# A new order for gates, key flips and route: one route tile with one key flip, gate copies later

## The chip, the cores and the metric

The kernel runs on one core of one Trainium2 chip. The metric is the device time of one execution in microseconds (us); lower is better. Engines are named as in the profile: PE is TensorE (PEld its weight loads), DVE is VectorE, ACT is ScalarE, POOL is GpSimd, SP is SyncE, which here only issues transfers.

## The reference

Eight batches of packed attention feed a mixture of experts with one expert per token, all in float32:

```
s  = scale * p @ k.T;  a = softmax(s);   p_packed = a @ v      # 32 packed queries per head
s2 = scale * q @ p_packed.T;  out = softmax(s2) @ p_packed      # 8 x 8 heads x 576 x 64
x  = out as rows (4608 x 512)
xn = x / (|x| + 1e-6);  en = emb / (|emb| + 1e-6)
logits = xn @ en.T / tau;  expert = argmax(logits);  gate = softmax(logits)[expert]
out[rows of e] = gate * (relu(x @ w1[e]) @ w2[e])               # 512 -> 1024 -> 512
```

## The kernel before

Each batch (576 tokens) has two parts. The attention part, `att_main(b)`, ends with the second softmax (`att2`), whose result is `AT`, the attention weights, transposed, as a high and a low half (`high`, `low`). The expert part, `ffn(b)`, guesses one expert for the whole batch, multiplies with its weights, and leaves tokens of other experts to a second pass at the end (none is taken in these inputs).

**Two programs woven by hand.** `ffn` is a generator that stops after every few matmuls, 56 stops for a usual batch: n = 0 to 15 are the hidden layer (`hidden`), n = 16 to 39 the transposed output rows of the last 320 tokens (line 943, four blocks `mt`), n = 40 to 55 the output tiles of the first 256 tokens (line 961, two tiles `c` of eight steps `f`). At each stop the loop at the end of the function takes one step of the next batch's attention (`step_att`), and from n = 28 (`GATE`) one step of this batch's gates (`gates_main`). For the first batch, which has 61 stops, an order written by hand, `PLAN`, says for each stop which steps to take: "a" is the second batch's attention, "k" one of its query flips, "g" gates, "r" the first batch's route, "w" and "W" the split of a weight tile on POOL or DVE, "q" and "s" steps of the first batch. The stop only sets where an instruction stands in its own engine's queue. Each engine then runs its queue in order, at its own pace.

**The steps around the change.** In the usual batch, attention's 32nd step is `turn(1)` on DVE; step 34 issues `low(1)`; steps 36 to 40 are the keys of the batch after next: `packers` and four `flip`s on DVE (three transposes each, lines 288 to 290); steps 41 to 45 are `route`. `route` has five tiles of tokens. Each takes a PSUM buffer `pt` of a pool of two, has six matmuls on PE (line 682), a small reduction on DVE (line 691) and a sum of squares on ACT (line 698), which frees the buffer. The reduction and the sum of one tile are issued one step after its matmuls.

`gates` makes the gate of each token of the batch: an inverse square root by small operations, mostly on POOL, then reciprocal and exponential on DVE and ACT (lines 744 to 755), then 16 small copies on ACT that spread the gates of the last 320 tokens (`spread_tail`, line 770). `store_tail` multiplies the transposed output by these (line 1269) and issues its output transfers; `turn_tail` (line 1260) brings each of the four `mt` blocks from PSUM on DVE.

The last attention (eighth batch) has no keys behind it, so its route comes five steps sooner. In the second batch (`early`) route starts one step after `turn(1)`, and its tiles alternate with the flips.

Of the kernel before, what the change touches and what calls it, by code (L numbers as in the profile page):

```python
# [23 lines left out]
def kernel(  # L24
# [12 lines left out]
    nc = tc.nc  # L37
# [3 lines left out]
    NG = H // HB  # L41
# [180 lines left out]
    def alternate(a, b):  # L222

        while a or b:
            for g in (a, b):
                if g:
                    try:
                        yield next(g)
                    except StopIteration:
                        a, b = (None, b) if g is a else (a, None)  # L230

    def idle(n):
        for _ in range(n):
            yield
# [190 lines left out]
    def rows_split(x, g):  # L425
        split([x.ppx[:, m, g, : HB * D] for m in range(2)], x.pp4[g].rearrange("p h d -> p (h d)"))
# [133 lines left out]
    def att2(x, after=None, first=False, early=False):  # L560

        def eng(name, hf):
            i = ("S0", "S1", "N0", "N1", "L0", "L1").index(name + str(hf))
            return nc.gpsimd if first and ENG[i] == "p" else nc.vector

        AT = sb.tile([P, 2, NG, S], F32R, name="AT", tag="AT")
        x.AT = AT
        NB = HS // 32
        both = slice(0, NG)
        sts, mxs, sums = [], [], []  # L570
        ats = x.ats = []

        def rows_of(t, gs):
            return t[:, gs].rearrange("p g (a j) -> p g a j", j=32)

        def spread(t, gs):
            n = gs.stop - gs.start
            return t[:, gs].unsqueeze(3).broadcast_to([P, n, NB, 32])

        def unpack(hf, gs=both):  # L580
            if gs.start == 0:
                sts.append(sb.tile([P, NG, HS], F32, name="st", tag="st", bufs=2))
            for g in range(gs.start, gs.stop):
                nc.vector.transpose(sts[hf][:, g], x.s2[hf][g])  # L584

        def biggest(hf, gs=both):
            if gs.start == 0:
                mxs.append(sm.tile([P, NG, NB], F32, name="mx2", tag="mx2", bufs=1))
            nc.vector.tensor_reduce(  # L589
                mxs[hf][:, gs], rows_of(sts[hf], gs), axis=AX.X, op=ALU.max  # L590
            )

        def shift(hf, gs=both):
            t = rows_of(sts[hf], gs)
            eng("S", hf).tensor_tensor(out=t, in0=t, in1=spread(mxs[hf], gs), op=ALU.subtract)  # L595

        def expo(hf, gs=both):
            nc.scalar.activation(sts[hf][:, gs], sts[hf][:, gs], AF.Exp, scale=SCALE)  # L598

        def total(hf, gs=both):  # L600
            if gs.start == 0:
                sums.append(sm.tile([P, NG, NB], F32, name="s2", tag="s2", bufs=1))
            t = sums[hf][:, gs]
            nc.vector.tensor_reduce(t, rows_of(sts[hf], gs), axis=AX.X, op=ALU.add)  # L604
            nc.vector.tensor_scalar(out=t, in0=t, scalar1=1e-9, scalar2=None, op0=ALU.add)
            nc.vector.reciprocal(t, t)

        def norm(hf, gs=both):
            t = rows_of(sts[hf], gs)
            eng("N", hf).tensor_tensor(out=t, in0=t, in1=spread(sums[hf], gs), op=ALU.mult)  # L610

        def turn(hf, gs=both):
            if gs.start == 0:
                if first and hf:
                    at = sb.tile([P, NG, HS], F32, name="at1", tag="ot", bufs=1)
                else:
                    at = sb.tile([P, NG, HS], F32, name="at", tag="at")
                ats.append(at)
            nc.vector.transpose(  # L619
                ats[hf][:, gs].rearrange("p g s -> p (g s)"),  # L620
                sts[hf][:, gs].rearrange("p g s -> p (g s)"),
            )

        def high(hf, gs=both):
            nc.scalar.copy(AT[:, 0, :, hf * HS : (hf + 1) * HS], ats[hf])  # L625

        def low(hf, gs=both):
            cs = slice(hf * HS, (hf + 1) * HS)
            eng("L", hf).tensor_tensor(
                out=AT[:, 1, :, cs], in0=ats[hf], in1=AT[:, 0, :, cs].bitcast(F32),  # L630
                op=ALU.subtract,
            )

        def softmax():
            order = (
                (unpack, 0), (biggest, 0), (shift, 0), (unpack, 1), (biggest, 1), (total, 0),
                (shift, 1), (norm, 0), (turn, 0), (total, 1), (low, 0), (norm, 1), (turn, 1),
            )
            if first:
                names = dict(  # L640
                    U=unpack, B=biggest, S=shift, X=expo, T=total, N=norm, R=turn, H=high, L=low
                )
                groups = {"": both, "a": slice(0, 1), "b": slice(1, 2)}
                order = [(names[t[0]], int(t[1]), groups[t[2:]]) for t in ORDS.split()]
            for step, hf, *gs in order:
                step(hf, *gs)
                if step is shift and not first:
                    expo(hf)
                if step is turn and not first:
                    high(hf)  # L650
                yield
            if first:
                return
            if early:

                steps = route(x)
                yield next(steps)
                low(1)
                yield
                yield from alternate(steps, after)  # L660
                return
            yield
            low(1)
            yield from idle(2)
            if after:
                yield from after

        yield from softmax()


# [61 lines left out]
        x.cnt = cnt  # L732


    def gates(x, eng=nc.vector):
        lg, ss = x.lg, x.ss
        y = sm.tile([P, NC5], F32, name="gy", tag="gy", bufs=1)
        for n, _ in enumerate(rsqrt(ss, y, "g", eng)):
            if n % 3 == 2:
                yield  # L740
        eng.tensor_tensor(out=y, in0=y, in1=ss, op=ALU.mult)
        eng.tensor_scalar(out=y, in0=y, scalar1=1e-6, scalar2=None, op0=ALU.add)
        yield
        nc.vector.reciprocal(y, y)
        nc.vector.tensor_tensor(
            out=lg, in0=lg, in1=y.unsqueeze(2).broadcast_to([P, NC5, E]), op=ALU.mult
        )

        nc.scalar.activation(lg, lg, AF.Exp)
        yield  # L750
        gate = sm.tile([P, NC5], F32, name="gate", tag="gate")
        nc.vector.tensor_reduce(gate.unsqueeze(2), lg, axis=AX.X, op=ALU.add)
        nc.vector.tensor_scalar(out=gate, in0=gate, scalar1=1e-9, scalar2=None, op0=ALU.add)
        yield
        nc.vector.reciprocal(gate, gate)  # L755

        x.gate = gate
        x.gt = sm.tile([P, NBT], F32, name="gt", tag="gt", bufs=1)
        yield
        for n, _ in enumerate(spread_tail(x.gt.unsqueeze(2), gate.unsqueeze(2), nc.scalar.copy)):  # L760
            if n % 4 == 3:
                yield
# [91 lines left out]
    def ffn(x, store, late=False, after=None, end=False):  # L854
# [99 lines left out]
        for c in range(NCT):  # L954

            w = 256 if end and c == NCT - 1 else 512
            for at in range(0, 512, w):
                pf = ps.tile([P, 512], F32, name="pf", tag="pf")
                for f in range(NF):
# [8 lines left out]
                    yield  # L968
                    if f == 0 and turning:
                        turn_tail(*turning.pop())  # L970
                    if f > 1:
                        next(tail, None)
                    if f == STF and last:
                        store(*last.pop(0))
# [50 lines left out]
    def att_main(b):  # L1025
        x = bat[b]
# [28 lines left out]
            load_w2(x, x.e, nc.gpsimd)  # L1055
        yield from second
        x.soft = True
        if b > 1:
            yield from route(x)
        if b == B - 1:  # L1060
            yield from idle(2)
            counts(x)
# [1 line left out]
    def begin():  # L1064
# [3 lines left out]
        x = bat[0]  # L1068
# [147 lines left out]
        yield  # L1216
        for g in range(NG):
            rows_split(x, g)
            yield
        x.begun = True  # L1220

    def keys_main(b):
        if b < B:
# [2 lines left out]

    def gates_main(b):
        x = bat[b]
        yield from gates(x, nc.gpsimd)
        hit = sm.tile([1, E], F32, name="hit", tag="hit")  # L1230
        nc.vector.tensor_tensor(out=hit, in0=x.cnt, in1=x.sel, op=ALU.mult)
        nc.vector.tensor_reduce(rest_f[:, b : b + 1], hit, axis=AX.X, op=ALU.add)

    def store_main(b):
# [60 lines left out]

    PLAN = (
        "qssq", "sssssssss", "sss", "ss", "ss", "ssG", "", "sG", "ssa", "ssa",
# [5 lines left out]
    )  # L1303
    DBL = 8
    LAG = 2

# [5 lines left out]
    with tc.manual_schedule():  # L1312
# [41 lines left out]
        for b in range(B):  # L1354
            after = bat[b + 1] if b + 1 < B else None
# [24 lines left out]
    with tc.If(n_rest > 0):  # L1380
        with tc.For_i(0, B, 1) as b:
            nb = nc.values_load(rest_i[0:1, ds(b, 1)], min_val=0, max_val=S)
            with tc.If(nb > 0):
                x = Batch()
# [97 lines left out]
```

## Time and profile before

| | |
|---|---|
| median of 3 runs | 490.4 us (488.78 to 492.2) |
| the profiled execution's own time | 490.11 us |
| its span, first to last instruction | 488.4 us |
| mean granted TensorE clock | 0.946 of full |
| PE, DVE, ACT, POOL busy | 90%, 62%, 45%, 36% |

The span and the trace are of the profiled execution; 1.7 us of its time lie outside the span. The trace's times are from the span's start. PEclk is the share of TensorE's full clock that was granted; it has two levels here, 1.0 (2.4 GHz) and 0.5 (1.2 GHz).

### The profile page before, as it was taken

How to read it: one execution, taken by the hardware profiler on the slowest of the kernel's cores; microseconds unless marked ns; L12 is line 12 of the kernel's file. 1: busy time of each engine (PE TensorE's matmuls, PEld its weight loads, DVE VectorE, ACT ScalarE, POOL GpSimd, SP SyncE). 2: the span in 40 equal slices, each digit the busy share in tenths (PEclk: the TensorE clock that was granted, in tenths of full speed). 3: DMA queues.
4: the chain of work that ended last, by engine and by line, in shares of the span. 5: the costliest groups of instructions: out<-in, count | busy, mean ns of one | idle time of the engine just before them, and what ended most of it. 6: DMA issues, size and time to landing. Idle time of an engine off the chain costs nothing.

```text
span 488.4 us, 10755 instructions
## 1 busy us (share of the span) xinstructions
PE 439.7 (90%) x3890; PEld 375.9 (77%) x3891; DVE 300.9 (62%) x874; ACT 219.2 (45%) x580; POOL 177.9 (36%) x303
## 2 busy tenths in 40 slices
PE   8799888999869996999959999599987999699994
PEld 5547778699857995788947989469976799679993
DVE  5487777477753887357963677547874488345330
ACT  2467425562246623474244721556234662437230
POOL 2456370343504353153512617044440535317200
PEclk9999997999979999899979999799997999799997
DMA  7999897758872588636973489725888203521022
GB/s 216 291 295 256 228 274 246 171 129 242 335 197 70 140 261 307 147 93 179 319 255 79 129 225 349 202 49 137 246 315 196 74 21 141 206 54 44 1 53 51
DMA packets 48860, 88.23 MB, mean 181 GB/s; under 512 B 11992, under 2 KB 30488, under 8 KB 48800
## 3 DMA queue, kind: packets, MB, share of 16 engines
q1 hardware_dynamic: 40512, 57.96, 44.8%
q0 software_dynamic: 8000, 29.43, 16.9%
q8 instruction: 32, 0.52, 0.5%
q14 instruction: 28, 0.23, 0.2%
q10 hardware_dynamic: 288, 0.08, 0.1%
HBM read 78.00 MB, written 9.44 MB: 179 GB/s over the span
## 4 chain that ended last, share of the span: by engine, by line
PE 59%; DVE 19%; DMA 8%; POOL 6%; issue 4%; ACT 1%; SPq 1%; DVEq 0%; ACTq 0%; POOLq 0%
PE pf L915 18%; PE pf L961 17%; PE pt L682 6%; PE pf L943 6%; DMA nat<-in_q 4%; DMA nat<-in_v 3%; PE pt L263 3%; PE pt L833 3%; POOL rq_t L106 2%; PE pt L388 2%; DVE st L584 2%; POOL rq_t L115 2%; DVE mx L589 2%; DVE s L604 2%; DVE st L595 2%
## 5 line engine op out<-in xcount | busy, mean ns | idle before, releaser
L809 POOL TENSOR_TENSOR w2s<-w2r,w2s 128x512 fp32r<-128x512 f32 x61 | 78.4, 1291 | 166.9 <-ACT w2s L808 86.0
L943 PE MATMUL pf<-hT,w2s 128*128 128x320 f32 x768 | 122.3, 315 | 0.0
L943 PEld LDWEIGHTS pf<-hT,w2s 128*128 128x128 f32 x768 | 115.4, 191 | 3.6 <-issue 3.3
L915 PE MATMUL pf<-AT,G 128*128 128x288 f32 x720 | 103.7, 298 | 0.1
L961 PE MATMUL pf<-w2s,hT 128*128 128x512 f32 (+1 forms) x408 | 101.1, 394 | 0.0
L915 PEld LDWEIGHTS pf<-AT,G 128*128 128x128 f32 x720 | 97.3, 188 | 4.7 <-issue 2.8
L961 PEld LDWEIGHTS pf<-w2s,hT 128*128 128x128 f32 x408 | 73.7, 196 | 18.4 <-issue 5.9
L682 PE MATMUL pt<-ppx,AT 128*128 128x264 f32 (+1 forms) x240 | 45.6, 336 | 33.6 <-ACT at L698 31.0
L918 DVE SCALAR_TENSOR_TENSOR hT<-pf,hT 128x288 fp32r<-128x288 f32 x128 | 56.4, 446 | 25.0 <-ACT hT L917 23.8
L682 PEld LDWEIGHTS pt<-ppx,AT 128*128 128x128 f32 (+1 forms) x240 | 41.5, 225 | 39.4 <-ACT at L698 33.4
L917 ACT ACTIVATE hT<-pf 128x288 fp32r<-128x288 f32 x128 | 51.4, 414 | 39.9 <-PE pf L915 38.4
L808 ACT CAST w2s<-w2r 128x512 fp32r<-128x512 f32 x64 | 39.1, 625 | 17.1 <-issue 15.2
L698 ACT ACTIVATE at<-pt 128x512 f32<-128x512 f32 (+1 forms) x40 | 23.9, 597 | 38.2 <-DVE lg L691 38.0
L847 DVE TENSOR_TENSOR G<-pt,G 128x512 fp32r<-128x512 f32 x28 | 19.4, 692 | 32.0 <-ACT G L846 32.0
L598 ACT ACTIVATE st<-st 128x576 f32<-128x576 f32 (+1 forms) x17 | 11.2, 660 | 51.5 <-DVE st L595 28.1
L770 ACT COPY gt<-gate 32x2 f32<-32x2 f32 (+1 forms) x128 | 24.6, 192 | 9.7 <-DVE gate L755 8.2
L691 DVE TENSOR_REDUCE lg<-pt 128x8 f32<-128x16 f32 (+1 forms) x40 | 5.8, 158 | 33.2 <-PE pt L682 33.2
L278 POOL TENSOR_TENSOR ppx<-pp,ppx 128x256 fp32r<-128x256 f32 x16 | 11.6, 741 | 40.2 <-ACT ppx L277 40.2
L846 ACT CAST G<-pt 128x512 fp32r<-128x512 f32 x28 | 16.5, 588 | 13.6 <-DVE G L847 10.6
L625 ACT CAST AT<-at 128x576 fp32r<-128x576 f32 x16 | 10.8, 674 | 26.1 <-DVE at L619 26.1
L1260 DVE STREAM_TRANSPOSE ot<-pf 128x320 f32<-128x320 f32 x32 | 15.9, 498 | 9.1 <-PE pf L943 9.1
L293 DVE STREAM_TRANSPOSE kt<-nat 128x576 f32<-128x576 f32 x28 | 21.4, 764 | 0.0
(174 smaller groups left out, 514.8 us busy)
## 6 DMA issues: line engine op xcount, KB each, us to landing
nat<-in_k SPq DMA_DIRECT2D x112, 140.0 KB, 3.2
nat<-in_q SPq DMA_DIRECT2D x112, 140.0 KB, 3.4
w1t<-in_moe_w POOLq DMA_DIRECT2D x14, 1024.0 KB, 8.3
w2r<-in_moe_w POOLq DMA_DIRECT2D x28, 512.0 KB, 10.9
nat<-in_v SPq DMA_DIRECT2D x32, 160.0 KB, 3.7
out<-ot SPq DMA_DIRECT2D x28, 160.0 KB, 3.2
nat<-in_v SPq DMA_DIRECT2D x32, 128.0 KB, 4.0
out<-o SPq DMA_DIRECT2D x60, 64.0 KB, 1.7
```

The costliest lines, as they stand in the source:

```text
L293: nc.vector.transpose(kt.rearrange("p (n i) -> p n i", i=32), t)
L682: nc.tensor.matmul(pt[:r, 512 * g : 512 * g + XW], AT[:, a, g, c * P : c * P + r], x.ppx[:, m, g], start=(i == 0), stop=(i == 2),)
L698: nc.scalar.activation(scr[:r, :, : HB * D], ptv[:r, :, 0 : HB * D], AF.Square, accum_out=ss[:r, c : c + 1])
L770: copy(dst[32 * a : 32 * a + 32, k : k + HB * (n - 1) + 1 : HB], src[32 * k : 32 * k + 32, NCT : NCT + n],)
L808: nc.scalar.copy(hi, raw)
L809: eng.tensor_tensor(out=lo, in0=raw, in1=hi.bitcast(F32), op=ALU.subtract)
L847: nc.vector.tensor_tensor(out=x.G[:, 1, g, fs], in0=src, in1=x.G[:, 0, g, fs].bitcast(F32), op=ALU.subtract,)
L915: nc.tensor.matmul(pf[:, :HS], w, r, start=(n == 0), stop=(n == len(ops) - 1))
L917: nc.scalar.activation(hT[:, 0, f, cs], pf[:, :HS], AF.Relu)
L918: nc.vector.scalar_tensor_tensor(out=hT[:, 1, f, cs], in0=pf[:, :HS], scalar=0.0, in1=hT[:, 0, f, cs].bitcast(F32), op0=ALU.max, op1=ALU.s ...
L943: nc.tensor.matmul(pf[:, : S - TL], x.w2s[f][:, m, mt * P : mt * P + P], hT[:, a, f, TL:], start=(n == 0), stop=(n == len(ops) - 1),)
L961: nc.tensor.matmul(pf[:, :w], hT[:, a, f, c * P : (c + 1) * P], x.w2s[f][:, m, at : at + w], start=(f == 0 and i == 0), stop=(f == NF - 1 ...
```

## The change

1. `gates` gets `lag`: for all batches but the first, three empty steps are put between the POOL part and the DVE reciprocal. So the 16 copies stand three stops later in ACT's queue, at n = 39 to 42 instead of 36 to 39.
2. The end of `att2`: before, the keys (`packers` and four flips) came first and route behind them. Now seven empty steps come behind `low(1)`, then `packers` and the first flip, then the five route tiles, each of the first three followed by one flip. Route's matmuls stay at n = 40 to 44. `att_main` no longer calls route itself. For the eighth batch, which has no keys behind it, route moves from n = 35..39 to n = 40..44.
3. In the second batch the same order holds with two empty steps (before: route tile, `low(1)`, then route tiles and keys in turn). Its `shift(1)` and `norm(1)` go from DVE to POOL (`POOLED`).
4. `store_tail` starts at step f = 6 of the first output tile (before: f = 2), and in the first batch only in the second output tile.
5. `PLAN` follows: in the first batch the gates move from stops 33..44 of the list to 43..55; the query flips, weight splits and row splits at 17 to 27 move by a step.

```
         def eng(name, hf):
+            if early and name + str(hf) in POOLED:
+                return nc.gpsimd
...
-            if early:
-
-                steps = route(x)
-                yield next(steps)
-                low(1)
-                yield
-                yield from alternate(steps, after)
+            yield
+            low(1)
+            if not after:
                 return
-            yield
-            low(1)
-            yield from idle(2)
-            if after:
-                yield from after
+            yield from idle(2 if early else 7)
+            yield next(after, None)
+            yield next(after, None)
+            for _ in route(x):
+                next(after, None)
+                yield
+            yield from after
...
-    def gates(x, eng=nc.vector):
+    def gates(x, eng=nc.vector, lag=0):
...
         yield
+        yield from idle(lag)
         nc.vector.reciprocal(y, y)
...
-                    if f > 1:
+                    if f > 1 if c else f > 5 and not late:
                         next(tail, None)
...
-        if b > 1:
-            yield from route(x)
...
-            yield
-        x.begun = True
+            x.begun = g == NG - 1
+            yield
...
-        yield from gates(x, nc.gpsimd)
+        yield from gates(x, nc.gpsimd, 3 if b else 0)
...
     PLAN = (
         "qssq", "sssssssss", "sss", "ss", "ss", "ssG", "", "sG", "ssa", "ssa",
-        "a", "sa", "a", "GG", "w", "aq", "aq", "aqw", "aq", "aW",
-        "w", "aqW", "Wr", "wk", "rak", "aw", "rkr", "akr", "ra", "ra",
-        "ra", "ra", "ra", "ga", "ga", "ga", "ga", "ga", "ga", "ga",
-        "ga", "ga", "ga", "ga", "ga", "a", "a", "a", "a", "a",
-        "a", "a", "a", "a", "a", "a", "a", "", "", "",
+        "a", "sa", "a", "GG", "w", "aq", "aq", "a", "aq", "qw",
+        "aW", "wWa", "Wr", "wk", "rka", "kaw", "rkr", "ar", "ra", "ra",
+        "ra", "ra", "ra", "a", "a", "a", "a", "a", "a", "a",
+        "a", "a", "aa", "gaa", "ga", "ga", "ga", "ga", "ga", "ga",
+        "ga", "ga", "ga", "ga", "g", "g", "g", "g", "", "",
     )
+    POOLED = ("S1", "N1")
```

## Rows read from the trace of the kernel before

**Rows 1.** The page: its busy line, and the group of line 698.

```profile
PE 439.7 (90%) x3890; PEld 375.9 (77%) x3891; DVE 300.9 (62%) x874; ACT 219.2 (45%) x580; POOL 177.9 (36%) x303
...
L698 ACT ACTIVATE at<-pt 128x512 f32<-128x512 f32 (+1 forms) x40 | 23.9, 597 | 38.2 <-DVE lg L691 38.0
```

**Rows 2.** The answer for line 698: who waited for it (us, times).

```profile
  PE pt L682: 31.0, 6
```

**Rows 3.** Timeline, PE, route of the fifth batch: start, length, instructions, [idle before].

```profile
246.94 0.90 PE L682 MATMUL pt<-ppx,AT 128*128 128x264 f32 x6
247.67 0.85 PE L961 MATMUL pf<-w2s,hT 128*128 128x512 f32 x3
253.84 1.69 PE L682 MATMUL pt<-ppx,AT 128*128 128x264 f32 x6 [5.31 <-ACT at L698]
```

**Rows 4.** The chain that ended last, the same stretch: start, length, what.

```profile
251.39 0.33 DVE kt L288
```

**Rows 5.** Timeline, DVE and ACT, the same stretch.

```profile
246.82 0.19 DVE L744 RECIPROCAL gy<-gy 128x5 f32<-128x5 f32 x1 [1.56 <-POOL gy L742]
...
248.02 0.23 DVE L299 TENSOR_SCALAR pn<-pn 128x128 f32<-128x128 f32 x1
...
248.59 0.47 DVE L1260 STREAM_TRANSPOSE ot<-pf 128x320 f32<-128x320 f32 x1
248.70 3.25 ACT L770 COPY gt<-gate 32x3 f32<-32x3 f32 x16 [1.12 <-DVE gate L755]
248.98 0.40 DVE L288 STREAM_TRANSPOSE kt<-nat 128x256 f32<-128x256 f32 x1
...
252.10 0.11 DVE L1231 TENSOR_TENSOR hit<-cnt,sel 1x8 f32<-1x8 f32 x1
...
252.32 0.49 DVE L1260 STREAM_TRANSPOSE ot<-pf 128x320 f32<-128x320 f32 x1
252.75 0.20 DVE L691 TENSOR_REDUCE lg<-pt 128x8 f32<-128x16 f32 x2
```

**Rows 6.** Stretches: us; PE, PEld, DVE, ACT, POOL busy; PEclk, DMA share, GB/s.

```profile
248.53:251.26 2.73, 0.00 (x0) 0.00 (x0) 2.73 (x12) 2.42 (x13) 0.00 (x0) 1.00 0.20 53
251.26:253.84 2.58, 0.01 (x1) 0.01 (x1) 2.45 (x11) 1.48 (x7) 0.00 (x0) 0.50 0.89 261
253.84:258.08 4.24, 4.24 (x16) 3.95 (x17) 0.91 (x2) 1.35 (x4) 0.00 (x0) 0.50 0.99 244
...
71.45:74.57 3.12, 0.51 (x4) 0.30 (x3) 2.44 (x10) 0.74 (x2) 0.56 (x4) 0.87 1.03 280
```

**Rows 7.** Timeline, PE and DVE, route of the eighth batch.

```profile
417.00 0.74 PE L943 MATMUL pf<-hT,w2s 128*128 128x320 f32 x4
417.58 0.90 PE L682 MATMUL pt<-ppx,AT 128*128 128x264 f32 x6
...
421.85 0.19 DVE L755 RECIPROCAL gate<-gate 128x5 f32<-128x5 f32 x1
...
423.32 1.69 PE L682 MATMUL pt<-ppx,AT 128*128 128x264 f32 x6 [4.26 <-ACT at L698]
```

**Rows 8.** Timeline, PE and DVE, route of the second batch.

```profile
74.57 1.25 PE L682 MATMUL pt<-ppx,AT 128*128 128x264 f32 x4 [2.05 <-DVE AT L629]
...
77.47 0.17 DVE L691 TENSOR_REDUCE lg<-pt 128x8 f32<-128x16 f32 x1
...
81.05 0.90 PE L682 MATMUL pt<-ppx,AT 128*128 128x264 f32 x6
```

**Rows 9.** Groups by form, POOL: the 576 wide softmax step: busy, mean ns.

```profile
L610 POOL TENSOR_TENSOR st<-st,s 128x576 f32<-128x576 f32 x1 | 1.2, 1161 | 4.0 <-DVE s L606 4.0
```

**Rows 10.** Timeline, POOL and DVE, gates of the fourth batch.

```profile
243.41 0.20 POOL L106 TENSOR_TENSOR rq_t<-rq_h,gy 128x5 f32<-128x5 f32 x1
...
244.50 0.76 DVE L629 TENSOR_TENSOR AT<-at,AT 128x576 fp32r<-128x576 f32 x1 [0.74 <-ACT AT L625]
244.56 0.75 POOL L106 TENSOR_TENSOR rq_t<-rq_h,gy 128x5 f32<-128x5 f32 x1
```

More of the change, by code (lines that the diff above doesn't have):

```diff
@@ L653, in softmax @@
                 return
-            if early:
-                steps = route(x)
-                yield next(steps)
-                low(1)
-                yield
-                yield from alternate(steps, after)
-                return
             yield
             low(1)
-            yield from idle(2)
-            if after:
-                yield from after
+            if not after:
+                return
+            yield from idle(2 if early else 7)
[5 more added lines that the diff above has]
+            yield from after
         yield from softmax()
```

## The prediction

> **What bounds the kernel now.** I read the page's busy line first: PE works for 90% of the span, so only its gaps, or its slow stretches, can be gained [rows 1]. Then I asked which gaps are long. Line 682, route's matmuls, waited six times for line 698 on ACT, 31.0 us in all, 5.2 us each [rows 2]: one gap in each `ffn` from the second batch's to the seventh's. The timeline shows one in place: two route tiles run, three output matmuls end near 248.5, and the third tile starts at 253.84 after 5.31 us of idle [rows 3]. It needs a PSUM buffer that the first tile's sum of squares frees. That sum in turn started only when the first tile's reduction on DVE had ended: of 38.2 us of idle ahead of line 698, 38.0 ended so [rows 1]. So the question is why DVE came so late. The chain of waits stands on a key flip there, not on PE [rows 4], and the timeline of DVE gives the order [rows 5]: a wait for POOL's gates until 246.82, the gate arithmetic, `packers` at 248.02, a `turn_tail` at 248.59, four flips from 248.98 to 252.10, the hit count, the last `turn_tail`, and only at 252.75 the reduction. PE resumes 1.09 us behind that reduction's start. PE is ahead of DVE by the length of this queue.
>
> The gap has a second price. The granted clock was full in its first 2.73 us and half from 251.26 to 258.08, so that PE worked 4.24 us at 1.2 GHz instead of 2.4 GHz and lost some 2.1 us more [rows 6].
>
> **The usual batch (five of the six gaps).** Route's matmuls keep their place in PE's queue, so the gap still opens at 248.5. Ahead of the first reduction, DVE's queue loses four things. Two of four flips go behind it: (252.10 - 248.98) / 4 = 0.78 us each, 1.56 us. The hit count goes: 252.32 - 252.10 = 0.22 us. The earlier `turn_tail` (248.98 - 248.59 = 0.39 us) now stands ahead of the gate reciprocal, where DVE was idle for 1.56 us waiting for POOL [rows 5]; POOL's chain, not the DVE order, sets 246.82, so `lag` itself gains nothing on DVE. Sum 2.17 us: reduction at 250.58, PE back at 251.67, gap 3.1 us in place of 5.3.
>
> The 16 copies of `spread_tail` are 3.25 us of ACT [rows 5], 0.2 us each. Eight now stand ahead of the first sum of squares, four ahead of the second and four ahead of the third. The gate reciprocal moves from 248.52 to about 248.05, as `packers` goes behind it, so eight copies end near 249.9, before the reduction: hidden, 0.7 us to spare. The four ahead of each later sum (0.8 us) lie beside the 0.78 us flip that now stands ahead of the same tile's reduction. The third sum would end near 255.0 and PE, at half clock, asks for its buffer near there: nothing, or up to 0.5 us a batch at full clock.
>
> What the flips feed starts later by some 2 us: loads of the next queries into freed buffers. They are wanted some 20 us on, hence free. The multiply of `store_tail` (two of about 0.8 us) moves behind the route tail, into idle DVE time: free. Its transfers come later on SP, with nothing urgent behind: free.
>
> Now the clock. The fall came 2.7 us into this gap, and the earlier stretch 71.45 to 74.57, with 0.51 us of work in 3.12, ended lower too (0.87 in the mean) [rows 6]. A gap of 3.1 us is between these and nearest the second, so I take it that the clock falls as before, at 251.26, and returns at 258.08. Then PE works 258.08 - 251.67 = 6.4 us at half clock, not 4.24, and loses 3.2 us, not 2.1. Half of the gain goes back: 2.17 - 1.08 = 1.09 us, for five batches **5.5 us**. Bounds: 0.4 us a batch if the fall comes so late that all 6.82 us of it fall on work and the copies cost 0.5; 4.2 us if it doesn't come.
>
> **The eighth batch's route (sixth gap).** There are no flips here, and route moves behind 4 steps of four line-943 matmuls. PE now waits 4.26 us [rows 7]; the half clock there costs some 2.7 us more, as it ran on 5.4 us after PE's return. After the change PE first does those steps, 0.58 us each (417.58 - 417.00), and three output steps of 0.7, so that the first two route tiles end and the gap opens near 422.1, about 3.0 us later. But the gate reciprocal stands at 421.85, and now eight copies of 0.2 us come ahead of the first sum: it starts at 423.7 in place of 422.6, and PE is back at 424.5. Gap 2.4 us. If the clock falls near its end, all 6.82 us lie on work, 3.4 us lost: 4.26 + 2.7 - 2.4 - 3.4 = **1.2 us** gained. If it doesn't fall: 4.6 us.
>
> **The second batch, in the first `ffn`.** Today PE waits 2.05 us for `low(0)` and starts the third route tile at 81.05; the first reduction is at 77.47, not behind a flip [rows 8]. The change takes from DVE, ahead of that reduction, the gates (0.9 us of small instructions and a wait of 0.75 for POOL, less 0.25 that return) and two softmax steps (0.72 each, pitch 1.36 together): 2.8 us. It puts ahead of it `packers` and two flips, 2.1 us, and waits for POOL: the step there takes 1.16 us [rows 9], `turn(1)` must wait for it, and POOL and DVE hold each other up: a POOL gate step that takes 0.20 us took 0.75 beside a two-input DVE step that ended with it at 245.3 [rows 10]. I put 1.6 us on these waits. The reduction comes at 77.5 - 2.8 + 2.1 + 1.6 = 78.4, the third tile at 79.5. PE has by then done the tail blocks and has one output step (0.7 us) less behind it: 80.2 against 81.05, 0.8 us won. But it was idle from about 75.4, 4.1 us, so the low clock moves to some 78 to 85 and takes 2.7 us: a loss of **1.8 us**. Bounds: a gain of 0.8 us if the clock holds, a loss of 3.5 if the POOL steps cost double.
>
> The GPSIMD Engine Reference of the Trainium skill (section 8, Key points) says that GpSimd shares its SBUF interfaces with VectorE and contends with DVE instructions of two SBUF inputs. The trace agrees (0.75 us against 0.20, [rows 10]); by that rule `norm(1)` would start only behind `low(0)`, which the 1.6 us already holds.
>
> The query flips of the second batch each move ahead by a stop; one leaves the way of a reduction (0.8 us), another comes into the way of the copy to `T` (0.8 us): nothing, within 0.8 us either way.
>
> **Sum.** 5.5 + 1.2 - 1.8 = 4.9 us off the profiled execution's 490.11: 485.2. Its time is 0.3 us below the median of the runs, which themselves spread over 3.4 us; I say 485.0.
>
> **Rivals.**
> 1. *The clock holds.* If a gap of 3.1 us is short enough in some batches, each gives 3.1 us more than I counted. For it: the gap is 40% shorter. Against: 71.45 to 74.57 [rows 6]. Two such batches: 479 us; all five: 469 us.
> 2. *No nearer.* The first reduction is held by something that I take as covered, say DVE waiting longer for POOL's gates, so that the gap stays at 5 us. For it: 246.82 is set by POOL. Against: the flips stand on the chain [rows 4]. Then only the second batch's loss and the eighth's gain are left: about 490.5 us.
> 3. *Slower: the copies take the flips' place.* If the gate reciprocal came 0.7 us later than I put it, ACT's copies would stand ahead of every sum of squares; from there on each tenth costs a tenth, and the four copies ahead of the second and third sums cost up to 0.8 us each when PE is at full clock. With 2.2 us lost in a batch to copies and 1.8 us in the second: 490.1 + 5 x (2.2 - 1.1) + 1.8 - 1.2 = 496 us. The reciprocal hangs on POOL, whose steps stretch as in [rows 10]; against it speak the 0.7 us and the flips.
>
> **How the numbers follow.** Forecast (482 to 488.5 by the bounds of its clock terms): 0.55. Clock holds in two or more gaps (469 to 480): 0.2. No nearer (489 to 491.5): 0.17. Slower (493 to 498): 0.08. A range of 478.5 to 490.5 leaves out about half of the second case, a third of the third and the fourth. About 1%, 4.9 us, is what a measurement of this kernel can tell from no change; below 485.5 lie some 0.3 of the forecast's 0.55 and all of the second case, so faster 0.5, same 0.44, slower 0.06.
>
> **What would show it.** In each of five batches PE's wait ahead of the third route tile is 3.1 us, and the first line-691 reduction stands behind two flips, not four. In the eighth batch's route it is 2.4 us, ended by ACT behind eight copies. In the second batch a wait of some 4 us appears at about 75. PEclk has as many low stretches as before. I am wrong if the low stretches vanish (faster), if line 770's copies end later than the first reduction in the usual batch, or if a wait of over 1 us appears ahead of the fourth or fifth tile.

## The result: a gain some four times the forecast

The changed kernel takes **471.3 us** (median of 4 runs, 470.22 to 472.56) against 490.6 for the kernel before in the same set: ratio **0.961 [0.957, 0.965]**. The forecast was 485.0 with a range down to 478.5. The sign was right, the size was not: 19.3 us are gone, and the working found 4.9.

One fact must stand first. **Both texts ahead of the result place route wrongly.** They say that its matmuls stay at the stops n = 40 to 44. The two lines `yield next(after, None)` are two stops, one for `packers` and one for the first flip, so route stands at **n = 42 to 46**, two stops later than before, in the eighth batch seven later. This is one cause of the miss, and the first experiment takes it out.

The page of the kernel after, its busy line and the groups of lines 682 and 698 (busy us and mean ns of one; idle ahead and what ended it):

```profile
PE 435.1 (93%) x3890; PEld 370.8 (79%) x3891; DVE 301.1 (64%) x872; ACT 218.0 (46%) x580; POOL 179.8 (38%) x305
...
L682 PE MATMUL pt<-ppx,AT 128*128 128x264 f32 (+1 forms) x240 | 41.5, 316 | 18.5 <-ACT at L698 18.5
...
L698 ACT ACTIVATE at<-pt 128x512 f32<-128x512 f32 (+1 forms) x40 | 23.9, 597 | 33.2 <-DVE lg L691 32.7
```

Route's wait for line 698 fell from 31.0 us, in six gaps [rows 2], to 18.5 in seven (the second batch has one now). The idle time of ACT that the last line puts down to DVE stands ahead of other tiles' sums of squares; ahead of the one that ends the gap ACT isn't idle, as the rows below show. The timeline of PE in the usual batch that answers to [rows 3]:

```profile
236.19 2.26 PE L962 MATMUL pf<-w2s,hT 128*128 128x512 f32 x9
238.29 0.89 PE L682 MATMUL pt<-ppx,AT 128*128 128x264 f32 x6
239.01 0.86 PE L962 MATMUL pf<-w2s,hT 128*128 128x512 f32 x3
239.71 0.90 PE L682 MATMUL pt<-ppx,AT 128*128 128x264 f32 x6
240.45 0.85 PE L962 MATMUL pf<-w2s,hT 128*128 128x512 f32 x3
243.92 1.10 PE L682 MATMUL pt<-ppx,AT 128*128 128x264 f32 x6 [2.62 <-ACT at L698]
```

Nine output matmuls, three steps of `c`, now stand ahead of the first route tile: the two later stops. The gap is 2.62 us, where 3.1 was forecast. What ends it shows in the timeline of DVE and ACT (to be held against [rows 5]):

```profile
238.33 0.19 DVE L745 RECIPROCAL gy<-gy 128x5 f32<-128x5 f32 x1 [1.12 <-POOL gy L742]
...
239.78 3.25 ACT L771 COPY gt<-gate 32x3 f32<-32x3 f32 x16 [0.69 <-DVE gate L756]
...
242.19 0.14 DVE L691 TENSOR_REDUCE lg<-pt 128x8 f32<-128x16 f32 x1
...
243.06 0.60 ACT L698 ACTIVATE at<-pt 128x512 f32<-128x512 f32 x1
```

The first reduction comes 3.86 us behind the gate arithmetic's first reciprocal; before it was 252.75 - 246.82 = 5.93. That is 2.07 us nearer (2.17 forecast). But ACT doesn't start its sum of squares then: all **sixteen** copies stand ahead of it, not eight, and the last one ends at 243.04. So PE waits for ACT's own queue and no longer for DVE. The chain of waits says the same:

```profile
242.84 0.20 ACT gt L771
243.04 0.02 issue
243.06 0.41 ACT at L698
...
243.92 1.10 PE pt L682 x6
```

The clock is the larger surprise. The stretches of the same batch (columns as in [rows 6]):

```profile
241.30:243.92 2.62, 0.00 (x1) 0.00 (x0) 2.58 (x14) 2.46 (x12) 0.00 (x0) 1.00 0.46 144
243.92:244.65 0.73, 0.73 (x6) 0.73 (x7) 0.35 (x2) 0.67 (x2) 0.00 (x0) 1.00 0.84 258
244.65:248.06 3.41, 3.41 (x14) 3.02 (x13) 0.57 (x3) 0.82 (x3) 0.00 (x0) 0.50 0.94 249
```

The granted clock is full through the gap and for 0.73 us after PE's return, then 1.2 GHz for 3.41 us, where [rows 6] have 2.58 + 4.24 = 6.82. All five usual batches and the eighth have one stretch of 3.41; the second batch has none, where before it had one of 6.83 from 73.76. Another of 3.41 at 22.8, in the first batch, is new.

Where the 19.5 us of the two spans (488.4 and 468.9) come from, by the start of each batch's first output matmul (line 943 before, 944 after):

| stretch | before, us | after, us | gain | forecast |
|---|---|---|---|---|
| start of the span to the first batch's output | 50.06 | 49.62 | 0.4 | 0 |
| first `ffn` (the second batch's route) | 63.12 | 60.99 | 2.1 | -1.8 |
| five usual batches | 289.32 | 273.97 | 15.4 | 5.5 |
| the eighth batch's route | 53.16 | 50.46 | 2.7 | 1.2 |
| from the last output block's start to the end | 32.75 | 33.83 | -1.1 | 0 |

### The profile page after: what moved, and what is told of

It reads as the page before. It is cut to its first block, busy times and chain, and to the rows that moved or that the text cites. A ratio compares the mean times of both kernels' runs of the same rounds, so it can differ in the third digit from the quotient of the medians.

```text
span 468.9 us, 10740 instructions
## 1 busy us (share of the span) xinstructions
PE 435.1 (93%) x3890; PEld 370.8 (79%) x3891; DVE 301.1 (64%) x872; ACT 218.0 (46%) x580; POOL 179.8 (38%) x305
## 4 chain that ended last, share of the span: by engine, by line
PE 53%; DVE 17%; DMA 11%; ACT 6%; POOL 6%; issue 3%; SPq 1%; DVEq 0%; ACTq 0%; POOLq 0%
PE pf L916 18%; PE pf L962 16%; DMA nat<-in_k 6%; PE pt L682 5%; PE pf L944 4%; ACT gt L771 4%; PE pt L834 3%; PE pt L263 3%; PE pt L388 2%; POOL rq_t L106 2%; DVE s L606 2%; DVE st L597 2%; DVE st L586 2%; DVE mx L591 2%; POOL rq_t L115 2%
## 5 line engine op out<-in xcount | busy, mean ns | idle before, releaser
L944 PE MATMUL pf<-hT,w2s 128*128 128x320 f32 x768 | 118.9, 311 | 0.0
L944 PEld LDWEIGHTS pf<-hT,w2s 128*128 128x128 f32 x768 | 113.0, 188 | 3.6 <-issue 3.3
L962 PE MATMUL pf<-w2s,hT 128*128 128x512 f32 (+1 forms) x408 | 103.2, 397 | 0.0
L919 DVE SCALAR_TENSOR_TENSOR hT<-pf,hT 128x288 fp32r<-128x288 f32 x128 | 56.5, 447 | 26.5 <-ACT hT L918 25.2
L682 PE MATMUL pt<-ppx,AT 128*128 128x264 f32 (+1 forms) x240 | 41.5, 316 | 18.5 <-ACT at L698 18.5
L682 PEld LDWEIGHTS pt<-ppx,AT 128*128 128x128 f32 (+1 forms) x240 | 38.0, 206 | 25.4 <-ACT at L698 21.5
L848 DVE TENSOR_TENSOR G<-pt,G 128x512 fp32r<-128x512 f32 x28 | 19.3, 690 | 17.2 <-ACT G L847 17.2
L785 POOL DMA_DIRECT2D w1t<-in_moe_w x14 | 11.1, 794 | 26.9 <-DVE st L597 23.0
```

Of the source, the lines that this page charges most:

```text
L682: nc.tensor.matmul(pt[:r, 512 * g : 512 * g + XW], AT[:, a, g, c * P : c * P + r], x.ppx[:, m, g], start=(i == 0), stop=(i == 2),)
L848: nc.vector.tensor_tensor(out=x.G[:, 1, g, fs], in0=src, in1=x.G[:, 0, g, fs].bitcast(F32), op=ALU.subtract,)
L919: nc.vector.scalar_tensor_tensor(out=hT[:, 1, f, cs], in0=pf[:, :HS], scalar=0.0, in1=hT[:, 0, f, cs].bitcast(F32), op0=ALU.max, op1=ALU.s ...
L944: nc.tensor.matmul(pf[:, : S - TL], x.w2s[f][:, m, mt * P : mt * P + P], hT[:, a, f, TL:], start=(n == 0), stop=(n == len(ops) - 1),)
L962: nc.tensor.matmul(pf[:, :w], hT[:, a, f, c * P : (c + 1) * P], x.w2s[f][:, m, at : at + w], start=(f == 0 and i == 0), stop=(f == NF - 1 ...
```

## Experiments

The theory going in: the gain is the shorter gaps, which ACT's copies now end, and the shorter low stretches behind them. The rivals: the gain comes from route's later place on PE alone, from the tail's multiply, or from the second batch's steps. The kernel before took 489.9 to 490.6 us beside these runs; each ratio is against it.

**Route where the texts had it.** In the kernel after:

```
-            yield from idle(2 if early else 7)
+            yield from idle(2 if early else 5)
```

> The changed kernel with five empty steps in place of seven, so that keys and route of the third to eighth batch stand two stops earlier (route's first tile at n = 40, as in the kernel before and as the prediction assumed). Theory A (cover): the two output steps that PE no longer has ahead of the wait, 1.4 us, come back as idle in six batches; about 2 us a batch lost: 481 to 483 us, PE's wait ahead of the third route tile some 3.1 us. Theory B (the new order of flips and reductions alone makes the gain, the stop of route is free): 471 us.

Measured: 475.9 us, ratio 0.971 [0.967, 0.974]. The gaps are 3.11, 3.12, 3.25, 3.38 and 3.09, the forecast's 3.1, and as it said ACT has eight copies ahead and then waits for DVE. Timeline, ACT and DVE, of one usual batch:

```profile
240.05 1.63 ACT L771 COPY gt<-gate 32x3 f32<-32x3 f32 x8 [1.12 <-DVE gate L756]
...
241.89 0.14 DVE L691 TENSOR_REDUCE lg<-pt 128x8 f32<-128x16 f32 x1
...
242.12 0.60 ACT L698 ACTIVATE at<-pt 128x512 f32<-128x512 f32 x1 [0.45 <-DVE lg L691]
```

The clock is what the forecast missed: two of these gaps (3.11, 3.12) are followed by no low stretch at all and their batches take 54.2 us each; one (3.25) has 6.83 us of it and takes 56.5; the others have 3.41 and take 55.1 and 55.6. The batch with the full stretch gained 57.85 - 56.5 = 1.35 us, near the 1.09 forecast; the others gained 2.3 to 3.7.

**The kernel before with route two stops later.** Ahead of route in `att_main`:

```
         if b > 1:
+            yield from idle(2)
             yield from route(x)
```

> The kernel before with two empty steps ahead of route in the third to eighth batch: all flips still ahead of it, nothing else changed. Theory A (cover): the first reduction stays where it is, the wait falls from 5.3 to about 3.9 us, six times 1.4 us less, and up to 1 us a batch more if the low clock gets shorter: 477 to 483 us. Theory B: 490 us.

Measured: 490.3 us, 0.999 [0.997, 1.002]: nothing. The gaps are 4.85 to 5.01, not 3.9. The timeline of DVE and PE:

```profile
309.86 0.49 DVE L1261 STREAM_TRANSPOSE ot<-pf 128x320 f32<-128x320 f32 x1
310.46 0.83 DVE L1270 TENSOR_TENSOR ot<-ot,gt 128x640 f32<-128x640 f32 x1
311.20 0.17 DVE L691 TENSOR_REDUCE lg<-pt 128x8 f32<-128x16 f32 x1
...
312.33 1.69 PE L682 MATMUL pt<-ppx,AT 128*128 128x264 f32 x6 [4.88 <-ACT at L698]
```

Moved back two stops, the reduction falls behind the multiply of `store_tail` (line 1270), which costs it 0.74 us. The low stretches of the usual batches stay at 6.83, and the shorter gap leaves more of one to PE's work: in the batch shown 5.55 us behind the gap, where [rows 6] have 4.24. So 0.4 us less of gap is paid back at the low clock, and such a batch takes 58.0 to 58.2 us, no less than before (57.7 to 58.0).

**The tail's multiply as before**, in the kernel after:

```
-                    if f > 1 if c else f > 5 and not late:
+                    if f > 1 if c else f > 1 and not late:
```

> The changed kernel with the tail's multiply from step f = 2 of the first output tile again, for all batches but the first. Theory A: the multiply waits for the copies on ACT and stands ahead of the first reduction, which comes 1.7 us later, so the wait grows from 2.6 to about 3.7 us in six batches: 476 to 480 us. The prediction held this move to be free: 471 us.

Measured: 480.8 us, 0.980 [0.976, 0.983]; gaps of 3.49 to 3.76. The multiply again stands ahead of the first reduction, and itself waits for the copies (timeline, DVE):

```profile
247.04 0.83 DVE L1268 TENSOR_TENSOR ot<-ot,gt 128x640 f32<-128x640 f32 x1 [0.80 <-ACT gt L771]
247.79 0.17 DVE L691 TENSOR_REDUCE lg<-pt 128x8 f32<-128x16 f32 x1
```

So the gaps are 1.0 us longer. Three of the seven low stretches are 6.83 again, one of them in the second batch, which this edit leaves alone. By the medians, taking back this one edit loses 9.5 of the 19 us; of the 10.6 us between the two profiled executions, 8.2 lie in the batches that it touches and 2.7 in the first `ffn`. It is no side issue.

**The tail's multiply later still**, in the second half of the output alone (`if c and f > 1:`).

> The kernel after with the tail's two multiplies only in the second half of the output steps; the copies stay where they are. It is the one of the two edits of the kernel with the copies behind that is not about the copies. Theory: both multiplies stand behind all of route's reductions in the kernel after already, so moving them further gives nothing: 471 us, within 2, gap 2.6 us as before. Rival, the multiplies still cost something where they stand (they delay the reductions of the fourth and fifth tile or the top-1 steps): 468 us or less.

Measured: 471.8 us, 0.964 [0.961, 0.966], the same as the kernel after: once behind the reductions, its place is worth nothing more.

**All four flips ahead of route** in the usual batches, route at the stops of the kernel after:

```
+            if not early:
+                yield from idle(4)
+                yield from after
+                yield from route(x)
+                return
```

> The changed kernel, with all four flips ahead of the first route tile of the third to seventh batch, route at the same stops. Theory A with ACT's copies as the bound: the first reduction comes 1.56 us later, 0.7 us behind the copies, so the wait grows from 2.6 to some 3.5 us in five batches: 475 to 478 us. Theory B: the gain of these five batches goes: about 486 us.

Measured: 478.7 us, 0.976 [0.971, 0.980], with gaps of 3.29 to 3.53 in the five batches, four low stretches of 3.41 and one of 6.83. Timeline, DVE and ACT, of one of them:

```profile
243.12 0.15 DVE L761 RECIPROCAL gate<-gate 128x5 f32<-128x5 f32 x1
...
243.30 3.25 ACT L776 COPY gt<-gate 32x3 f32<-32x3 f32 x16 [1.52 <-DVE gate L761]
...
245.91 0.14 DVE L696 TENSOR_REDUCE lg<-pt 128x8 f32<-128x16 f32 x1
...
246.57 0.60 ACT L703 ACTIVATE at<-pt 128x512 f32<-128x512 f32 x1
```

The first reduction is over at 246.05, ahead of the copies' end at 246.55: in all five batches the copies end the gap here too. With `packers` and a flip ahead of the gate reciprocal in DVE's queue, they start 0.8 us later behind the gate arithmetic's first reciprocal (2.27 us, in the kernel after 1.45), and the gap is 0.8 us longer. So the expectation had the length of the gap right, but not that the reduction would end it. By the medians the old order loses 7.4 us; by the two profiled executions, 5.0 of 8.0 us lie in these five batches, the others mostly in the first `ffn` and the last block, which the edit leaves alone.

**Without the lag** (`gates(x, nc.gpsimd, 0)`).

> The kernel after without the three idle stops ahead of the gate reciprocal (`lag`). Theory: the reciprocal waits for POOL's gate steps wherever it stands (1.12 us of idle ahead of it at 238.33), so ACT's sixteen copies start near 239.8 as now and end near 243.0, and the gap stays at 2.6 us: 471 us, within 2. Rival, the lag carries part of the gain, because without it `turn_tail` and the key's packing stand behind that wait on DVE and push the first reduction past the copies: gap 3.2 us or more, 474 us or more.

Measured: 469.9 us, 0.958 [0.956, 0.960], gaps 2.48 to 2.78: the lag carries no gain, as the forecast said. ACT's copies take 240.82 to 244.07 there, and the sum of squares follows at 244.10.

**Only the usual batches' part, and only the second batch's.** The kernel after with the first `ffn` as before (`PLAN`, `POOLED`, the early order); and the kernel before with these alone changed.

> The changed kernel with the first ffn as before: the old PLAN, the second batch's old order of route, low(1) and keys, its steps on DVE, the first batch's tail as before. If the parts add up, it lacks the 2.8 us that the first ffn gains by the traces: 474 us. If the prediction's loss in the second batch were true (1.8 us), it would be faster than the whole change: 469 to 470 us.

> The kernel before with the first ffn alone changed: the new PLAN, the second batch's new order, shift(1) and norm(1) on POOL, the first batch's tail in the second output tile. If the parts add up: 487.5 us, PE's wait in the second batch about 3.1 us and no low clock there. By the prediction's step: 492 us.

Measured: 472.5 us, 0.963 [0.960, 0.965], and 490.5 us, 1.001 [0.999, 1.004]. The usual part is the whole of what can be measured. In the trace of the second one the first `ffn` takes 62.5 us, where the table has 63.1 before and 61.0 after. Its execution has a low stretch of 3.41 us at 78.31, behind a gap of 3.16, and that of the kernel after has none: half of 3.41 is the 1.5 between them, but for 0.2.

**The gap filled with matmuls.** The kernel before with 20 idle multiplications of the identity ahead of the third route tile; they add work and leave what PE waits for as it was:

```
+                    if c == 0 and f == 2 and not late and after is not None:
+                        fl = ps.tile([P, 512], F32, name="fl", tag="pf")
+                        for _ in range(20):
+                            nc.tensor.matmul(fl[:, :P], ident, ident, start=True, stop=True)
```

> The kernel before with 20 matmuls of 128 by 128 (the identity with itself, into a PSUM buffer that nobody reads) ahead of the third route tile of the third to seventh batch, some 4 us of PE work in a wait of 5.3 us. If the low clock costs what the prediction put on it, 2.1 us a batch, and work in the wait keeps the clock: 480 us, no low stretch in five batches. If the low clock costs nothing, 490 us.

Measured: 484.5 us, 0.989 [0.986, 0.991]. Timeline of PE:

```profile
300.41 4.63 PE L971 MATMUL fl<-ident 128*128 128x128 f32 x40
305.90 1.01 PE L682 MATMUL pt<-ppx,AT 128*128 128x264 f32 x6 [0.86 <-ACT at L698]
```

(The trace has two rows for each of the twenty.) PE is back 0.86 + 4.63 = 5.49 us behind the fillers' start, no sooner than with the gap of 5.3 (0.14 to 0.17 us later in the five batches), yet the clock stays full from 5.3 to 411.5 us and a usual batch takes 56.0 us, not 57.85. So the low clock behind one gap costs **1.85 us**, or some 2.0 if PE's later return is added (2.1 in the forecast). The `ffn` with the eighth batch's route lost 4.1 us: the fillers come behind that route there and meet no gap. That is why the whole stays above the 480 us expected.

**The copies behind route.** Two edits in the kernel after: five empty stops ahead of the copies, and the multiply in the second half alone, since it reads what the copies write.

```
+        yield from idle(back)      # gates: back = 5 for b > 0
         for n, _ in enumerate(spread_tail(...)):
...
-                    if f > 1 if c else f > 5 and not late:
+                    if c and f > 1:
```

> The changed kernel, with five more empty steps ahead of the 16 copies of gates, so that they stand behind the first two sums of squares, and the tail's multiply in the second output tile for every batch. If ACT's copies end the wait now (theory A), PE comes back with the first reduction: the wait is some 2.0 us in the usual batch and near 0 in the eighth, 466 us with the clock as it is and 456 to 460 us if it no longer falls. If the copies are not the bound, 471 us.

Measured: **462.2 us**, 0.943 [0.938, 0.948]. The second edit alone gave nothing (above), so this is the copies. Timeline, DVE, ACT and PE:

```profile
294.63 0.20 DVE L290 STREAM_TRANSPOSE kt<-nat 128x64 f32<-128x64 f32 x1
294.76 0.13 DVE L691 TENSOR_REDUCE lg<-pt 128x8 f32<-128x16 f32 x1
...
294.99 0.60 ACT L698 ACTIVATE at<-pt 128x512 f32<-128x512 f32 x1 [3.33 <-DVE lg L691]
...
295.73 1.00 PE L682 MATMUL pt<-ppx,AT 128*128 128x264 f32 x6 [2.03 <-ACT at L698]
```

ACT is free 3.33 us early; the reduction behind `packers` and two flips ends the gap, of 1.72 to 2.03 us, and the eighth batch, which has no flips, has none.

**Route ahead of the keys as well**, on top of that:

```
+            yield from idle(9)
+            for i, _ in enumerate(route(x)):
+                if i:
+                    next(after, None)
```

> The kernel with the copies behind route, and route's first tile moved ahead of the key's packing and its first flip as well; a key's step comes with each tile from the second on. Theory: the first reduction is what ends the gap in that kernel (it ran 1.09 us after it could), and with nothing but the gates ahead of it on DVE the sum of squares starts in time: gaps under 1 us in the five usual batches, no low stretch there, 454 us, between 450 and 458. Rival one, the flips are then late for what they feed and the time comes back behind them: 462 us or more, with a new wait ahead of the keys or of the next queries. Rival two, DVE still waits for POOL's gates ahead of the first reduction: gaps stay at 1.7 us, 462 us.

Measured: **449.0 us** (448.1 to 449.66), 0.916 [0.913, 0.918]. It beats both kernels, and the 454 us expected. Its group of route's matmuls:

```profile
L690 PE MATMUL pt<-ppx,AT 128*128 128x264 f32 (+1 forms) x240 | 36.8, 291 | 3.2 <-ACT at L706 3.1
```

and the timeline of DVE in a usual batch, with the reduction now ahead of `packers`:

```profile
232.91 0.48 DVE L1268 STREAM_TRANSPOSE ot<-pf 128x320 f32<-128x320 f32 x1
233.31 0.14 DVE L699 TENSOR_REDUCE lg<-pt 128x8 f32<-128x16 f32 x1
233.37 0.21 DVE L299 TENSOR_SCALAR pn<-pn 128x128 f32<-128x128 f32 x1
```

The 3.1 us left are the second batch's gap, whose order this kernel leaves alone. The usual batches have no gap and no low stretch, and take 50.7 us: 7.1 less than before. That is the whole price of a gap as read above, 5.3 of idle and 1.85 of low clock. The flips, a few stops later now, delay nothing that shows.

**That kernel with the copies ahead again** (`back` = 0).

> The last kernel with one thing put back: ACT's sixteen copies stand ahead of route's first sum of squares, as in the kernel after, while route's first reduction stays ahead of the key's packing and flips. Theory, the copies alone set the gap of the kernel after: the first reduction ends even earlier than there (242.2 in the kernel after), and the sum of squares still starts only when the copies have ended, 3.3 us after they began; gaps of 2.4 to 2.8 us in the five usual batches, a low stretch of 3.41 us in each, near 470 us, between 467 and 473. Rival, DVE's order counted too in the kernel after: gaps of 1.7 us or less and 462 us or less.

Measured: 472.7 us, 0.966 [0.961, 0.970], gaps of 2.47 to 2.77. Timeline, ACT, DVE and PE:

```profile
240.53 3.25 ACT L780 COPY gt<-gate 32x3 f32<-32x3 f32 x16 [0.69 <-DVE gate L764]
240.81 0.14 DVE L699 TENSOR_REDUCE lg<-pt 128x8 f32<-128x16 f32 x1
...
243.81 0.60 ACT L706 ACTIVATE at<-pt 128x512 f32<-128x512 f32 x1
...
244.67 1.00 PE L690 MATMUL pt<-ppx,AT 128*128 128x264 f32 x6 [2.62 <-ACT at L706]
```

The reduction ran at 240.81 and the sum of squares still starts at 243.81, when the copies end. So in the kernel after the copies alone set the gap. DVE's order costs something there only where it makes the copies start later (all flips first) or puts a step that waits for them ahead of the reduction (the tail's multiply as before); by itself it counts once they are out of the way.

## Why the prediction was right or wrong

**What bounds the kernel: right.** The gap ahead of the third route tile, and the clock behind it, were worth 7.1 us a batch by the kernel with route ahead of the keys: the 5.3 us of gap in the trace of before and the 1.85 that the fillers show (the working had 2.1 for it).

**Route's place: wrong, a misreading of the code.** "Route's matmuls keep their place in PE's queue" fails by two stops. With it fail "eight now stand ahead of the first sum of squares" (sixteen do) and "hidden: 0.7 us to spare" (the copies end 0.7 us behind the reduction's end, 243.04 against 242.33). Two more output steps on PE outweigh that: 2.62 us of gap, not 3.1. With route at the stops of the text, the gap is 3.1 and the copies have 0.45 us to spare, so the DVE sum (2.17 forecast, 5.93 - 3.72 = 2.21 there, and 2.07 in the kernel after) and the copies' price held for the kernel that was costed. The two stops are worth 475.9 - 471.3 = 4.6 us by the medians; the trace has 1.6 of it in the five usual batches, but it is that of the fastest of the four runs (473.0).

**The clock: the term that was mis-sized most.** "I take it that the clock falls as before, at 251.26, and returns at 258.08" is the step that failed. Per usual batch the forecast had the low clock cost 1.1 us more than before; it costs about 3.41 / 2 = 1.7 us after and 1.85 before, so a little less. Of the 1.98 us by which each of the five batches beat the forecast (3.07 against 1.09), this is 1.2 to 1.5, and the shorter gap 0.5. Even at the forecast's own gap of 3.1 us only one batch of the five had the 6.83 us stretch. The prediction took the length of a low stretch as a fixed 6.82 us; the batches of before had no other, and that was no bound.

**Rival 1, the clock holds:** its time for all five, 469 us, is near the result, but not its mechanism. The clock still falls in every usual batch; the stretch is half as long.

**The tail's multiply: "free" was wrong for the place where route really stands.** There the old place is ahead of the first reduction and costs 1.0 us of gap and longer low stretches, 9.5 us by the medians. In the kernel before the same multiply stands right behind the first two reductions (252.92 in the fifth batch). A step called free was free only at one distance to its neighbour. What was not priced was the order of this multiply to the reduction.

**`lag` gains nothing: right** (469.9 us without it).

**The eighth batch:** the gap forecast (2.4 us, ended by ACT behind copies) came out at 2.47, but by luck: sixteen copies stand ahead instead of eight, which ends the gap later, and route stands at n = 42, which opens it later. With route at the text's n = 40 it is 2.25, behind eight copies as forecast. The gain was 2.7 us, not 1.2, since 3.41 us of low clock fall on PE's work and not 6.82: by half of that, 1.7 us are lost and not 3.4. The step is again the clock.

**The second batch: the waits about right, the clock left to the execution.** First reduction 77.91 (78.4 forecast), third tile 78.88 (79.5), gap 3.15 (4.1). "So the low clock moves to some 78 to 85 and takes 2.7 us" failed for the trace of after, which has no low stretch there. Ten kernels here have the new first `ffn`, all with a gap of 3.14 to 3.17 us in it. In their traces it takes 61.0 to 61.5 us in three without a low stretch, 62.3 to 62.8 in six with 3.41 us of it, and 63.7 in the one with 6.83 (the tail's multiply as before, from 77.34). The old order takes 63.1 with 6.83, and 62.3 with 3.41 or none. So the 2.1 us of the table are for the greater part the luck of one execution; where the stretch came in full, as forecast, the new order lost 0.6 us, not 1.8. The median of that part alone (490.5 us) shows neither a gain nor a loss.

The contention was there: `norm(1)` on POOL took 1.48 us where [rows 9] have 1.16, beside a DVE step of two inputs (`low(0)`, line 631). Timeline, POOL and DVE, of the kernel after:

```profile
67.17 1.15 POOL L597 TENSOR_TENSOR st<-st,mx 128x576 f32<-128x576 f32 x1 [0.55 <-DVE mx L591]
67.77 0.59 DVE L607 TENSOR_SCALAR s<-s 128x18 f32<-128x18 f32 x1
...
71.14 0.18 DVE L607 TENSOR_SCALAR s<-s 128x18 f32<-128x18 f32 x1
...
71.54 0.69 DVE L631 TENSOR_TENSOR AT<-at,AT 128x576 fp32r<-128x576 f32 x1
71.76 1.48 POOL L612 TENSOR_TENSOR st<-st,s 128x576 f32<-128x576 f32 x1 [3.45 <-DVE s L608]
...
73.27 0.78 DVE L621 STREAM_TRANSPOSE at<-st 128x576 f32<-128x576 f32 x1 [1.04 <-POOL st L612]
```

The same DVE step of line 607 takes 0.59 us while POOL works, ending at 68.36 as POOL's step does (68.32), and 0.18 without it. The GPSIMD Engine Reference of the Trainium skill (section 8, Key points) names contention with DVE instructions in a 2-port mode beside those with two inputs. The trace agrees for two inputs, with 1.48 us against 1.16; the step of line 607 has one input and is held up too, but no run here shows in which mode it ran. That `norm(1)` would start only behind `low(0)` isn't shown: its row begins at 71.76, inside `low(0)`'s (71.54 to 72.23). What line 607 took longer (0.41 us) and DVE's wait for POOL ahead of line 621 (1.04) are 1.45 us, near the 1.6 set aside.

**Rival 2, no nearer,** didn't come: the flips and the packing were on the path. **Rival 3, the copies in the flips' place,** came true in its mechanism (ACT ends all six gaps, and line 770's copies, now line 771, end behind the first reduction, a sign of being wrong that the prediction named), though by route's later stops and not by a late reciprocal. Its price did not come, as the reciprocal came in time and PE had two steps more.

**Left open:** why the last block gives 1.1 us back. The loss lies behind PE's last matmul (8.3 us to the end, 7.2 before), and SP's issues of output rows take longer there (5.78 us for eight, 4.38 before; in the kernel without the lag 4.38 again, with a block of 33.1 us), but no run took this apart. Nor was it settled what decides between no stretch, 3.41 us and 6.83 us behind gaps of nearly one length.

## What to carry to other kernels

When a queue is reordered, name for each engine what will stand ahead of the releasing step afterwards, and count the stops in the code one by one. Here DVE's flips, DVE's multiply and ACT's copies were three covers over one gap, each worth nothing or much by which of the others was still there; only when all three went behind route did the whole 7.1 us of a batch come. And look which step ends the wait before naming the one that was moved: the flips, put back in front, lengthened the gap by making the copies start later. Work that nobody waits for soon, such as the copies and flips, belongs behind the step that frees a buffer for the bounding engine.

A low-clock stretch behind a gap is a cost that can shrink with the gap: price it from both ends, and if it matters, fill the gap with dummy matmuls once and read what the clock alone costs.

## What was unexpected of the hardware

Gaps of PE ahead of the third route tile and the stretch at 1.2 GHz with them: 5.3 us, 6.83 (all five of before; in the kernel with the second batch's part alone, 3.41 once behind such a gap); 4.85 to 5.01, 6.83; 3.49 to 3.76, 3.41 or 6.83; 3.29 to 3.53, 3.41 four times, 6.83 once; 3.14 to 3.17 in the second batch, none three times, 3.41 six times, 6.83 once; 3.09 to 3.38, none twice, 3.41 twice, 6.83 once; 2.47 to 2.78, 3.41; 1.72 to 2.03, 3.41 in three and none in two; without a gap, none. The fall often comes only when PE is back at work, as at 244.65, 0.73 us behind its return. So a shorter gap makes the fall rarer and shorter, and its length alone doesn't decide.
